# First and last K block loaded in halves, unread TensorE products, and softmax denominators moved ahead, in a cached attention decode kernel

## The chip, the cores and the metric

The kernel runs on one core of one Trainium2 chip. The metric is device microseconds of one launch, as the median of several runs. Beside the runs there is one profiled execution, from which all rows below come; times in it are counted from the first instruction, and the span reaches to the last one.

## The reference

Two tokens (B = 2, one step each, D = 512) pass through attention with a cached K and V of 8192 positions, 32 heads of 128, and the result is gated by a small MLP:

```python
xn = layernorm(x)
q = (xn @ wq)                       # 2 x 32 heads x 128
scores = q . k_cache * Dh**-0.5     # 2 x 32 x 8192
p = softmax(scores)
o = p . v_cache
s = o.reshape(2, 1, 4096) @ wo
g = silu(gelu(layernorm(xn) @ w1 + b1) @ w2 + b2)
return x + s * g
```

Everything is float32. K and V are 268 MB each, wo and wq 8.4 MB each: every byte is used once.

## The kernel before, in words

The 64 (token, head) pairs are taken two at a time, in N = 32 rounds. In a round, partitions 0 to 63 hold one head's 8192 positions (128 each) and partitions 64 to 127 the other's; a round's K, and its V, is one block of 128 partitions x 128 positions x 128 numbers, 8.4 MB. There are three such buffers, `big[0..2]`: two for K (`KBUF`), one for V (`VB`). The setup uses `big[2]` for the MLP weights and `big[1]` for wq; in the end the last V (number 31) goes into `KBUF[0]`, and wo into `VB`.

The order on each engine is written out by hand. Semaphores carry the dependences: `op` issues one instruction with its waits, `take` waits on a semaphore and counts it down. The code of almost every instruction is in the helper `op` (L51 in the rows), so rows are told apart by tiles.

- SP issues all large transfers into one queue: the MLP weights, wq, K 0, K 1 (after the product with wq, L265), V 0 (L288), and then in round n the block K n+2, which waits until VectorE is through with K n (`k_done`, L297), and V n+1, which waits until TensorE is through with V n (`p_v`, L298). In round 30 come the two halves of V 31, each with its own semaphore (L301), and in L302 to L305, after the product with V 30, wo in seven pieces (`WO_CUTS`).
- VectorE in round n: K times the query in place (L276), the sum over the 128 numbers of each position (L277), the maximum of each partition `MX` (L279), and, from TensorE's transpose of `MX`, the negated maximum of each head `nm` (L280). It does the next K only after `nm`.
- TensorE in round n (`softmax`, `weighted`): the transpose of `MX`, the product that spreads `nm` over the partitions (`pn`), then 32 products of the exponentials `PZ` with V (two records each in the trace, on four groups of 32 output rows), and four products that bring the result O into columns (`pt`). Its 31 rounds after the first are a loop on the engine (L412); the last V is done by `weighted(KBUF[0], last=True)`, which waits for each half of V 31 before the products that read it.
- ScalarE copies `pn` to `bias`, makes the exponentials with their sums (`RS`), and copies O out of PSUM (`o4`, `OT`).

After the last round VectorE makes `Z` (O spread for the gathering product, L310) and `ZL` (the sums `RS` spread likewise, L313); TensorE makes from them the unnormalised rows and the denominators in `OA` (L417 to L421); VectorE takes the reciprocal of the denominators `rl` (L315) and normalises (`on`, L316). Then TensorE runs 128 products with wo (256 records, L422), waiting for each piece of wo where it is first read, and VectorE gates the sum, adds x (`res`, L318) and the result is stored.

Of the kernel before, what the change touches and what calls it, by code (L numbers as in the profile page):

```python
# [4 lines left out]
AF = mybir.ActivationFunctionType  # L5
ALU = mybir.AluOpType
AX = mybir.AxisListType
# [6 lines left out]
class Program:  # L14
# [24 lines left out]
    def wait(self, eng, *tokens):  # L39
        for name, v in self.need(eng, tokens):  # L40
            self.engines[eng].wait_ge(self.sem(name), v)

    def take(self, eng, name, v=1):

        self.engines[eng].wait_ge(self.sem(name), v).then_inc(self.sem(name), -v)  # L45

    def op(self, eng, method, *args, waits=(), sig=None, quiet=False, **kwargs):
        need = self.need(eng, waits)
        for name, v in need[:-1]:
            self.engines[eng].wait_ge(self.sem(name), v)  # L50
        ins = getattr(self.engines[eng], method)(*args, **kwargs)  # L51
        for name, v in need[-1:]:
            ins._wait_ge(self.sem(name), v)
        if quiet:
            return None
        name = sig or "own_" + eng
        by = 16 if method == "dma_start" else 1
        ins.then_inc(self.sem(name), by)
        self.counts[name] += by
        return name, self.counts[name]  # L60


def decode_kernel(nc, x, kc, vc, wq, wo, w1, b1, w2, b2, out):
    P = 128
    B, H, S, DH = kc.shape
# [17 lines left out]
    PH = P // H  # L83
    OC = DH // PH
    BH = B * H
    NPB = 512 // DH
    WO_CUTS = (0, 10, 18, 24, 28, 30, 31, 32)
    V_CUTS = (0, KP // 2, KP)

    pr = Program(nc)  # L90
    op, wait, take = pr.op, pr.wait, pr.take
# [7 lines left out]
    kf = kc.rearrange("b h s d -> (b h s d)").rearrange("(n p j d) -> n p j d", p=P, j=KP, d=DH)  # L99
# [4 lines left out]
    KBUF, VB = rows[:2], rows[2]  # L104
# [32 lines left out]
    z = sb([P, P], "z")  # L137
# [6 lines left out]
    SC = [sb([P, KP], f"sc{i}") for i in range(2)]  # L144
# [42 lines left out]
    op("SP", "dma_start", b1_sb[:, NF:], b1[F - P:, None], sig="d_b")  # L187
    t["b"] = op("SP", "dma_start", b2_sb, b2[None, :], sig="d_b")
    op("SP", "dma_start", wq_sb, wq.rearrange("(p c) n -> p c n", p=P), sig="d_wq")
    k_land = {0: op("SP", "dma_start", KBUF[0], kf[0], sig="d_k0")}  # L190
    t["x4m"] = op("DVE", "memset", x4, 0.0)
    for b in range(B):
        t["x4"] = op("ACT", "dma_start", x4[b::R, :], x[b, 0].rearrange("(j n) -> j n", n=P), sig="d_x4",
# [68 lines left out]
    t["th"] = op("ACT", "activation", th, z, AF.Tanh, scale=0.5, waits=[t["z"]])  # L262


    op_k1 = op("SP", "dma_start", KBUF[1], kf[1], sig="d_k1", waits=[pe("pq"), ("d_wq", 16)])  # L265
    k_land[1] = op_k1

    pending = {}
    for n in range(N):
        k = KBUF[n % U]  # L270
        if n:

            op("ACT", "copy", o4, po, sig="s_o4", waits=[pe_n("p_v", n - 1)])
            t["OT"] = op("ACT", "copy", OT[:, U * (n - 1):U * n], pt[:, :U], waits=[pe_n("p_t", n - 1)])
        qb = Q[:, n, :].unsqueeze(1).to_broadcast([P, KP, DH])
        a = op("DVE", "tensor_tensor", out=k, in0=k, in1=qb, op=ALU.mult, waits=[k_land[n], Qt[n]])  # L276
        a = op("DVE", "tensor_reduce", out=SC[n % 2], in_=k, axis=AX.X, op=ALU.add, waits=[a], sig="v_k")  # L277
        k_done = a
        op("DVE", "tensor_reduce", out=MX, in_=SC[n % 2], axis=AX.X, op=ALU.max, waits=[a], sig="v_mx")  # L279
        op("DVE", "tensor_reduce", out=nm, in_=pm[:1, :P].rearrange("o (s r) -> o s r", s=U), axis=AX.X,  # L280
           op=ALU.max, negate=True, waits=[pe_n("p_m", n)], sig="v_nm")
        if n == 0:
            a = op("DVE", "scalar_tensor_tensor", gate, th, 1.0, z, op0=ALU.add, op1=ALU.mult,
                   waits=[t["th"], t["pool"]])
            t["gate"] = a

            wait("SP", t["sel"], t["qnat"], pe("pgate"))
            op("SP", "dma_start", VB, vf[0], sig="d_v")  # L288
        a = op("ACT", "copy", bias, pn[:, :1], waits=[pe_n("p_n", n)])
        sc = SC[n % 2].rearrange("p (t j) -> p t j", j=JW)  # L290
        for s in range(U):
            r = slice(HP * s, HP * (s + 1))
            op("ACT", "activation", PZ[r, :, s, :], sc[r], AF.Exp, bias=bias[r], scale=SCALE,
               accum_out=RS[r, n:n + 1], waits=[a, t["pool"]], sig="s_pz")
        m = n + 2
        if m < N:
            k_land[m] = op("SP", "dma_start", KBUF[m % U], kf[m], sig=f"d_k{m % U}", waits=[k_done])  # L297
            op("SP", "dma_start", VB, vf[m - 1], sig="d_v", waits=[pe_n("p_v", m - 2)])  # L298
        elif m == N:
            for i, (c0, c1) in enumerate(zip(V_CUTS, V_CUTS[1:])):  # L300
                op("SP", "dma_start", KBUF[m % U][:, c0:c1], vf[N - 1][:, c0:c1], sig=f"d_v31{i}", waits=[k_done])  # L301
            wait("SP", pe_n("p_v", N - 2))  # L302
            wo_v = wo.rearrange("(p c) n -> p c n", p=P)
            for i, (c0, c1) in enumerate(zip(WO_CUTS, WO_CUTS[1:])):
                op("SP", "dma_start", wo_sb[:, c0:c1], wo_v[:, c0:c1], sig=f"d_wo{i}")  # L305
    op("ACT", "copy", o4, po, sig="s_o4", waits=[pe_n("p_v", N - 1)])
    t["OT"] = op("ACT", "copy", OT[:, U * (N - 1):], pt[:, :U], waits=[pe_n("p_t", N - 1)])

    shape = [P, BH, PH]
    op("DVE", "tensor_tensor", out=Z, in0=blk.unsqueeze(1).to_broadcast(shape),  # L310
       in1=OT.unsqueeze(2).to_broadcast(shape), op=ALU.mult, waits=[t["OT"], t["blk"]])
    shape = [P, N, U * PH]
    t["Z"] = op("DVE", "tensor_tensor", out=ZL, in0=half.unsqueeze(1).to_broadcast(shape),  # L313
                in1=RS.unsqueeze(2).to_broadcast(shape), op=ALU.mult, waits=[t["half"]])
    a = op("DVE", "reciprocal", rl, OA[:, :, OC], waits=[pe_n("p_oa", 0)])  # L315
    t["on"] = op("DVE", "tensor_tensor", out=on, in0=OA[:, :, :OC], in1=rl.unsqueeze(2).to_broadcast([P, B, OC]),  # L316
                 op=ALU.mult, waits=[a])
# [11 lines left out]
    def mm(dst, w, v, start=True, stop=True, sig=None, waits=(), skip=False):  # L329
        kw = {"skip_group_check": True} if skip else {}  # L330
        if sig in PE_EVENTS:
            done.append(sig)
            sig = "pe_setup"
        return op("PE", "matmul", dst, w, v, start=start, stop=stop, waits=waits, sig=sig, quiet=sig is None, **kw)
# [49 lines left out]
           waits=[t["b"]], sig="pgate" if j == QT - 1 else None)  # L384
    assert done == PE_EVENTS, done

    def softmax():
        take("PE", "v_mx")
        op("PE", "transpose", pm[:1, :P], MX, ident, sig="p_m")
        take("PE", "v_nm")  # L390
        for s in range(U):
            mm(pn[HP * s:HP * (s + 1), :1], srow, nm[:, s:s + 1], sig="p_n" if s == U - 1 else None)

    def weighted(v, last=False):
        take("PE", "s_pz", U)
        if not last:
            take("PE", "d_v", 16)
        for i in range(NT):
            if last and i * JW in V_CUTS:
                nc.tensor.wait_ge(pr.sem(f"d_v31{V_CUTS.index(i * JW)}"), 16)  # L400
            j = i % QT
            mm(po[R * j:R * j + U * JW, :], PZ[:, i].rearrange("p s j -> p (s j)"),
               v[:, i * JW:(i + 1) * JW, :].rearrange("p j d -> p (j d)"), start=i < QT, stop=i + QT >= NT,
               sig="p_v" if i == NT - 1 else None)
        take("PE", "s_o4")
        for i in range(JW):
            mm(pt[:, :U], o4[:, i * DH:(i + 1) * DH], mod[:, i:U * JW:JW], start=i == 0, stop=i == JW - 1,
               sig="p_t" if i == JW - 1 else None)

    wait("PE", t["mem"], t["pool"], t["mod"])  # L410
    softmax()
    with nc.tensor.Fori(0, N - 1):  # L412
        weighted(VB)
        softmax()
    weighted(KBUF[0], last=True)

    for b in range(B):  # L417
        h = slice(b * H, (b + 1) * H)
        mm(OA[:, b, :OC], Z[:, h].rearrange("p h r -> p (h r)"), mod, waits=[t["Z"]])
        m = slice(b * HH, (b + 1) * HH)  # L420
        mm(OA[:, b, OC:], ZL[:, m].rearrange("p n r -> p (n r)"), ones[:, :1], sig="p_oa" if b == B - 1 else None)  # L421
# [32 lines left out]
```

## Time and profile before

| | us |
|---|---|
| median of 3 runs (lowest, highest) | 1304.08 (1302.92, 1304.64) |
| profiled execution, its own time | 1304.39 |
| its span | 1303.1 |
| VectorE busy | 1129.3 (87%) |
| TensorE busy | 404.0 (31%) |
| ScalarE busy | 70.5 (5%) |
| bytes moved, mean rate over the span | 559.5 MB, 429 GB/s |

The profile is one page of sums and a trace that can be asked for a stretch of time. A row of the timeline has the start, the duration, the engine, the line, the operation with its tiles and shapes, and in brackets how long the engine had been idle before it and what ended that. "PEld" is TensorE's weight load, "SPq" the issue of a transfer. The mean TensorE clock granted in the span was 0.633 of the full one. Of a transfer the trace has the time from its issue to its landing.

### The profile page before, as it was taken

Reading aid. Unit: us, or ns where it says so; the run is one execution under the profiler, and the core shown is the slowest. Engines: PE = TensorE matmul, PEld = TensorE weight load, DVE = VectorE, ACT = ScalarE, POOL = GpSimd, SP = SyncE. Lnnn points to the kernel's source line nnn. Section 1 sums busy time; section 2 is a strip of 40 time slices with the busy share of each in tenths; the row PEclk is TensorE's granted clock in tenths of the full one; section 3 lists DMA queues with packets and bytes.
Section 4 is the critical chain, followed back from the end, with each engine's and each line's share of the span. In section 5 each row is a group of like instructions: output and inputs, shape, how many; then the busy total and the mean of one; then the engine's idle time right before and its main releaser. Section 6 shows DMA issues by size and latency. Waiting matters only on the chain. (4 is left out here: it accounts for less than half of the span.)

```text
span 1303.1 us, 7007 instructions
## 1 busy us (share of the span) xinstructions
PE 404.0 (31%) x3128; PEld 147.0 (11%) x3128; DVE 1129.3 (87%) x166; ACT 70.5 (5%) x244; POOL 1.1 (0%) x8
## 2 busy tenths in 40 slices
PE   6602333212333311333321233221233331133337
PEld 6300010000001000100000010000011000001103
DVE  2299999998889988888988888988888998888891
ACT  1200000000000000000000000000000000000000
POOL 0000000000000000000000000000000000000000
PEclk9956666556666656666656666655666655666667
DMA  9999999999999999999999999999999999999997
GB/s 401 444 424 437 429 437 431 433 433 435 433 431 437 433 437 433 435 433 437 428 439 429 439 429 435 433 431 437 431 439 431 437 431 439 429 439 429 439 420 311
DMA packets 11280, 559.51 MB, mean 429 GB/s; under 512 B 1523, under 2 KB 1539, under 8 KB 2054
## 3 DMA queue, kind: packets, MB, share of 16 engines
q1 hardware_dynamic: 11242, 559.36, 99.4%
q8 instruction: 6, 0.10, 0.0%
q14 instruction: 4, 0.03, 0.0%
q10 hardware_dynamic: 28, 0.01, 0.0%
HBM read 559.37 MB, written 0.00 MB: 429 GB/s over the span
## 5 line engine op out<-in xcount | busy, mean ns | idle before, releaser
L51 DVE TENSOR_TENSOR big<-big,Q 128x16384 f32<-128x16384 f32 x32 | 551.1, 17222 | 102.1 <-DMA big<-in_A_k_cache_dram 77.1
L51 DVE TENSOR_REDUCE sc<-big 128x128 f32<-128x16384 f32 x32 | 551.0, 17220 | 1.1
L51 PE MATMUL bank<-big,PZ 128*8 128x512 f32 x2048 | 293.0, 736 | 618.3 <-PEq L45 618.3
L51 PEld LDWEIGHTS bank<-big,PZ 128*8 128x8 f32 x2048 | 60.7, 103 | 823.7 <-issue 823.7
L51 PE MATMUL bank<-ident,MX 128*1 128x128 f32 x32 | 11.9, 371 | 217.8 <-PEq L45 217.8
L51 ACT COPY o<-bank 128x512 f32<-128x512 f32 x32 | 18.7, 585 | 874.0 <-PE bank L51 874.0
L51 PE MATMUL bank<-mod,o 128*128 128x2 f32 x256 | 32.8, 250 | 25.6 <-PEq L45 25.6
L51 PEld LDWEIGHTS bank<-mod,o 128*128 128x128 f32 x256 | 31.0, 191 | 54.4 <-issue 54.4
L51 PEld LDWEIGHTS bank<-ident,MX 128*1 128x1 f32 x32 | 2.5, 79 | 219.8 <-issue 219.8
L51 ACT ACTIVATE PZ<-sc,bias 64x128 f32<-64x128 f32 x64 | 25.5, 399 | 1.9
L51 DVE TENSOR_REDUCE nm<-bank 1x2 f32<-1x128 f32 x32 | 8.9, 278 | 17.8 <-PE bank L51 17.8
L51 PE MATMUL bank<-yT,big 128*128 128x2 f32 x88 | 19.9, 364 | 0.8 <-DMA big<-in_B_w_dram 0.8
L51 PEld LDWEIGHTS bank<-yT,big 128*128 128x128 f32 x88 | 19.9, 321 | 0.9 <-DMA big<-in_B_w_dram 0.9
L51 DVE TENSOR_TENSOR gh<-bank,b_sb 128x22 f32<-128x22 f32 x1 | 0.2, 182 | 21.6 <-PE bank L51 21.6
L51 ACT COPY bias<-bank 128x1 f32<-128x1 f32 x32 | 5.1, 159 | 250.9 <-PE bank L51 250.9
L51 PE MATMUL bank<-nm,srow 1*64 1x1 f32 x128 | 12.0, 243 | 14.8 <-PEq L45 14.8
L51 PEld LDWEIGHTS bank<-nm,srow 1*64 1x64 f32 x128 | 10.2, 200 | 24.1 <-issue 24.1
L51 DVE TENSOR_TENSOR Z<-blk,OT 128x256 f32<-128x256 f32 x1 | 0.4, 424 | 13.9 <-ACT OT L51 13.9
L51 PE MATMUL bank<-big,xnT 128*2 128x512 f32 x64 | 9.7, 773 | 7.3 <-DMA big<-in_A_wq_dram 7.3
L51 ACT ACTIVATION_READ_ACCUMULATOR PZ<-sc,bias 64x1 f32 x64 | 11.8, 185 | 0.0
L51 DVE TENSOR_REDUCE MX<-sc 128x1 f32<-128x128 f32 x32 | 9.2, 286 | 1.1
L51 PE MATMUL bank<-big,on 128*2 128x128 f32 x256 | 9.2, 317 | 0.6 <-DVE on L51 0.6
(65 smaller groups left out, 65.7 us busy)
## 6 DMA issues: line engine op xcount, KB each, us to landing
big<-in_A_v_cache_dram SPq DMA_DIRECT2D x2, 4096.0 KB, 37.9
big<-in_B_w_dram SPq DMA_DIRECT2D x1, 2752.0 KB, 9.4
big<-in_B_w_dram SPq DMA_DIRECT2D x1, 2560.0 KB, 14.8
big<-in_A_wo_dram SPq DMA_DIRECT2D x1, 2560.0 KB, 16.6
big<-in_A_wo_dram SPq DMA_DIRECT2D x1, 2048.0 KB, 21.1
big<-in_A_wo_dram SPq DMA_DIRECT2D x1, 1536.0 KB, 24.3
big<-in_A_wo_dram SPq DMA_DIRECT2D x1, 1024.0 KB, 25.9
big<-in_A_k_cache_dram SPq DMA_DIRECT2D x32, 42.9
```

The source lines that it names most:

```text
L51: ins = getattr(self.engines[eng], method)(*args, **kwargs)
```

## The change

There are three parts.

1. K 0 and K 31 are loaded by two transfers each, of half the positions, with a semaphore for each half (`load_k`, `K_CUTS`); VectorE multiplies and sums each half by itself. The other K blocks stay whole. V 31 was in halves before.
2. `unread(4, 2)` and the like issue TensorE products of the identity with 512, 256 or 128 columns of the queries `Q` into bank 6, which nobody reads. They stand in every round before the transpose of `MX` (twice 512 columns) and before the `nm` product (128 columns), and in the end before the last exponentials, between the halves of V 31, before the O transposes, before the `OA` products and before the wo products. The first one also waits until the gate has been copied out of bank 6.
3. `ZL`, the two products that make the denominators, and their reciprocal are put ahead: VectorE makes `ZL` after the last `nm`, as soon as the last exponentials are done, TensorE makes the denominators right after the last V products (`p_den`), and the reciprocal follows. `Z`, the two row products and the normalisation stay where they were.

```diff
-    V_CUTS = (0, KP // 2, KP)
+    HALVES = (0, KP // 2, KP)
+    WHOLE = (0, KP)
+    K_CUTS = {0: HALVES, N - 1: HALVES}
...
+    def load_k(n, *waits):
+        cuts = K_CUTS.get(n, WHOLE)
+        k_land[n] = [op("SP", "dma_start", KBUF[n % U][:, a:b], kf[n][:, a:b], sig=f"d_k{n % U}{i}", waits=waits)
+                     for i, (a, b) in enumerate(zip(cuts, cuts[1:]))]
...
-        a = op("DVE", "tensor_tensor", out=k, in0=k, in1=qb, op=ALU.mult, waits=[k_land[n], Qt[n]])
-        a = op("DVE", "tensor_reduce", out=SC[n % 2], in_=k, axis=AX.X, op=ALU.add, waits=[a], sig="v_k")
+        cuts = K_CUTS.get(n, WHOLE)
+        for i, (c0, c1) in enumerate(zip(cuts, cuts[1:])):
+            qb = Q[:, n, :].unsqueeze(1).to_broadcast([P, c1 - c0, DH])
+            a = op("DVE", "tensor_tensor", out=k[:, c0:c1], in0=k[:, c0:c1], in1=qb, op=ALU.mult,
+                   waits=[k_land[n][i], Qt[n]])
+            a = op("DVE", "tensor_reduce", out=SC[n % 2][:, c0:c1], in_=k[:, c0:c1], axis=AX.X, op=ALU.add,
+                   waits=[a], sig="v_k")
...
+    t["ZL"] = op("DVE", "tensor_tensor", out=ZL, in0=half.unsqueeze(1).to_broadcast(shape),
+                 in1=RS.unsqueeze(2).to_broadcast(shape), op=ALU.mult, waits=[t["pz"], t["half"]])
+    t["rl"] = op("DVE", "reciprocal", rl, OA[:, :, OC], waits=[pe_n("p_den", 0)])
     op("ACT", "copy", o4, po, sig="s_o4", waits=[pe_n("p_v", N - 1)])
...
-    t["Z"] = op("DVE", "tensor_tensor", out=ZL, in0=half.unsqueeze(1).to_broadcast(shape),
-                in1=RS.unsqueeze(2).to_broadcast(shape), op=ALU.mult, waits=[t["half"]])
-    a = op("DVE", "reciprocal", rl, OA[:, :, OC], waits=[pe_n("p_oa", 0)])
+    t["Z"] = op("DVE", "tensor_tensor", out=Z, in0=blk.unsqueeze(1).to_broadcast(shape),
+                in1=OT.unsqueeze(2).to_broadcast(shape), op=ALU.mult, waits=[t["OT"], t["blk"]])
...
+    def unread(*heads):
+
+        for n in heads:
+            mm(bank[6][:, :n * DH], ident, Q[:, :n, :].rearrange("p n d -> p (n d)"), waits=[t["z"], t["Q0"]])
+
     def softmax():
+        unread(4, 4)
         take("PE", "v_mx")
         op("PE", "transpose", pm[:1, :P], MX, ident, sig="p_m")
+        unread(1)
         take("PE", "v_nm")
...
-        take("PE", "s_pz", U)
+        if last:
+            unread(4, 2)
+            wait("PE", t["pz"])
+        else:
+            take("PE", "s_pz", U)
...
+            if last and i * JW == HALVES[1]:
+                unread(2)
...
+        if last:
+            for b in range(B):
+                m = slice(b * HH, (b + 1) * HH)
+                mm(OA[:, b, OC:], ZL[:, m].rearrange("p n r -> p (n r)"), ones[:, :1], waits=[t["ZL"]],
+                   sig="p_den" if b == B - 1 else None)
+            unread(1)
         take("PE", "s_o4")
...
     weighted(KBUF[0], last=True)
+    unread(2)
...
+    unread(1)
     for i, (c0, c1) in enumerate(zip(WO_CUTS, WO_CUTS[1:])):
```

More of the change, by code (lines that the diff above doesn't have):

```diff
@@ L189, in decode_kernel @@
     op("SP", "dma_start", wq_sb, wq.rearrange("(p c) n -> p c n", p=P), sig="d_wq")
-    k_land = {0: op("SP", "dma_start", KBUF[0], kf[0], sig="d_k0")}
+    def load_k(n, *waits):
+        cuts = K_CUTS.get(n, WHOLE)
+        k_land[n] = [op("SP", "dma_start", KBUF[n % U][:, a:b], kf[n][:, a:b], sig=f"d_k{n % U}{i}", waits=waits)
+                     for i, (a, b) in enumerate(zip(cuts, cuts[1:]))]
+    k_land = {}
+    load_k(0)
     t["x4m"] = op("DVE", "memset", x4, 0.0)
@@ L262, in decode_kernel @@
     t["th"] = op("ACT", "activation", th, z, AF.Tanh, scale=0.5, waits=[t["z"]])
-    op_k1 = op("SP", "dma_start", KBUF[1], kf[1], sig="d_k1", waits=[pe("pq"), ("d_wq", 16)])
-    k_land[1] = op_k1
+    load_k(1, pe("pq"), ("d_wq", 16))
     pending = {}
@@ L274, in decode_kernel @@
             t["OT"] = op("ACT", "copy", OT[:, U * (n - 1):U * n], pt[:, :U], waits=[pe_n("p_t", n - 1)])
-        qb = Q[:, n, :].unsqueeze(1).to_broadcast([P, KP, DH])
-        a = op("DVE", "tensor_tensor", out=k, in0=k, in1=qb, op=ALU.mult, waits=[k_land[n], Qt[n]])
-        a = op("DVE", "tensor_reduce", out=SC[n % 2], in_=k, axis=AX.X, op=ALU.add, waits=[a], sig="v_k")
+        cuts = K_CUTS.get(n, WHOLE)
[5 more added lines that the diff above has]
+                   waits=[a], sig="v_k")
         k_done = a
@@ L292, in decode_kernel @@
             r = slice(HP * s, HP * (s + 1))
-            op("ACT", "activation", PZ[r, :, s, :], sc[r], AF.Exp, bias=bias[r], scale=SCALE,
-               accum_out=RS[r, n:n + 1], waits=[a, t["pool"]], sig="s_pz")
+            t["pz"] = op("ACT", "activation", PZ[r, :, s, :], sc[r], AF.Exp, bias=bias[r], scale=SCALE,
+                         accum_out=RS[r, n:n + 1], waits=[a, t["pool"]], sig="s_pz" if n < N - 1 else None)
         m = n + 2
         if m < N:
-            k_land[m] = op("SP", "dma_start", KBUF[m % U], kf[m], sig=f"d_k{m % U}", waits=[k_done])
+            load_k(m, k_done)
             op("SP", "dma_start", VB, vf[m - 1], sig="d_v", waits=[pe_n("p_v", m - 2)])
         elif m == N:
-            for i, (c0, c1) in enumerate(zip(V_CUTS, V_CUTS[1:])):
+            for i, (c0, c1) in enumerate(zip(HALVES, HALVES[1:])):
                 op("SP", "dma_start", KBUF[m % U][:, c0:c1], vf[N - 1][:, c0:c1], sig=f"d_v31{i}", waits=[k_done])
@@ L305, in decode_kernel @@
                 op("SP", "dma_start", wo_sb[:, c0:c1], wo_v[:, c0:c1], sig=f"d_wo{i}")
+    shape = [P, N, U * PH]
+    t["ZL"] = op("DVE", "tensor_tensor", out=ZL, in0=half.unsqueeze(1).to_broadcast(shape),
+                 in1=RS.unsqueeze(2).to_broadcast(shape), op=ALU.mult, waits=[t["pz"], t["half"]])
+    t["rl"] = op("DVE", "reciprocal", rl, OA[:, :, OC], waits=[pe_n("p_den", 0)])
     op("ACT", "copy", o4, po, sig="s_o4", waits=[pe_n("p_v", N - 1)])
@@ L309, in decode_kernel @@
     shape = [P, BH, PH]
-    op("DVE", "tensor_tensor", out=Z, in0=blk.unsqueeze(1).to_broadcast(shape),
-       in1=OT.unsqueeze(2).to_broadcast(shape), op=ALU.mult, waits=[t["OT"], t["blk"]])
-    shape = [P, N, U * PH]
-    t["Z"] = op("DVE", "tensor_tensor", out=ZL, in0=half.unsqueeze(1).to_broadcast(shape),
-                in1=RS.unsqueeze(2).to_broadcast(shape), op=ALU.mult, waits=[t["half"]])
-    a = op("DVE", "reciprocal", rl, OA[:, :, OC], waits=[pe_n("p_oa", 0)])
+    t["Z"] = op("DVE", "tensor_tensor", out=Z, in0=blk.unsqueeze(1).to_broadcast(shape),
+                in1=OT.unsqueeze(2).to_broadcast(shape), op=ALU.mult, waits=[t["OT"], t["blk"]])
     t["on"] = op("DVE", "tensor_tensor", out=on, in0=OA[:, :, :OC], in1=rl.unsqueeze(2).to_broadcast([P, B, OC]),
-                 op=ALU.mult, waits=[a])
+                 op=ALU.mult, waits=[t["rl"], pe_n("p_oa", 0)])
     a = op("DVE", "scalar_tensor_tensor", res, acc, 0.5, gate, op0=ALU.mult, op1=ALU.mult,
@@ L398, in weighted @@
         for i in range(NT):
-            if last and i * JW in V_CUTS:
-                nc.tensor.wait_ge(pr.sem(f"d_v31{V_CUTS.index(i * JW)}"), 16)
+            if last and i * JW == HALVES[1]:
+                unread(2)
+            if last and i * JW in HALVES:
+                nc.tensor.wait_ge(pr.sem(f"d_v31{HALVES.index(i * JW)}"), 16)
             j = i % QT
@@ L408, in weighted @@
                sig="p_t" if i == JW - 1 else None)
-    wait("PE", t["mem"], t["pool"], t["mod"])
+    wait("PE", t["mem"], t["pool"], t["mod"], t["z"])
     softmax()
@@ L415, in decode_kernel @@
     weighted(KBUF[0], last=True)
+    unread(2)
     for b in range(B):
         h = slice(b * H, (b + 1) * H)
-        mm(OA[:, b, :OC], Z[:, h].rearrange("p h r -> p (h r)"), mod, waits=[t["Z"]])
-        m = slice(b * HH, (b + 1) * HH)
-        mm(OA[:, b, OC:], ZL[:, m].rearrange("p n r -> p (n r)"), ones[:, :1], sig="p_oa" if b == B - 1 else None)
+        mm(OA[:, b, :OC], Z[:, h].rearrange("p h r -> p (h r)"), mod, waits=[t["Z"]],
+           sig="p_oa" if b == B - 1 else None)
+    unread(1)
     for i, (c0, c1) in enumerate(zip(WO_CUTS, WO_CUTS[1:])):
```

## The prediction

> **What bounds the kernel now.** I read the page first, then the chain that ended last, then the timeline of the last 70 us with the landings of its transfers, and the TensorE clock microsecond by microsecond. All times are us from the start of the span.
>
> ```profile
> span 1303.1 us, 7007 instructions
> q1 hardware_dynamic: 11242, 559.36, 99.4%
> L51 DVE TENSOR_TENSOR big<-big,Q 128x16384 f32<-128x16384 f32 x32 | 551.1, 17222 | 102.1 <-DMA big<-in_A_k_cache_dram 77.1
> ```
>
> One queue carries 559.36 MB and fills 99.4% of the span of the 16 DMA engines. VectorE waits 77.1 us for K. So the body of the kernel is the transfer stream, and only what stands after the stream's last byte, or what makes the stream pause, can change the time.
>
> The end is different. The chain view, its last 16 us (start, duration, what):
>
> ```profile
> 1287.82 0.42 DVE Z L51
> 1288.25 0.35 DVE ZL L51
> ...
> 1288.64 1.88 PE bank L51 x8
> ...
> 1290.55 0.18 DVE rl L51
> ...
> 1290.75 0.24 DVE on L51
> ...
> 1291.12 9.27 PE bank L51 x256
> 1300.41 0.30 DVE res L51
> ```
>
> The last piece of TensorE is the product with wo: 256 records without a pause, up to 1300.4. The issue rows and the landings of the last two pieces of wo (us from issue to landing; the second landing row is the median of both):
>
> ```profile
> 1269.12 0.43 SPq L51 DMA_DIRECT2D big<-in_A_wo_dram  x1
> 1269.59 0.43 SPq L51 DMA_DIRECT2D big<-in_A_wo_dram  x1
> big<-in_A_wo_dram SPq DMA_DIRECT2D x1, 256.0 KB, 27.0
> big<-in_A_wo_dram SPq DMA_DIRECT2D x2, 256.0 KB, 27.2
> ```
>
> The sixth piece lands at 1269.12 + 27.0 = 1296.1; the median 27.2 makes the seventh 27.4, so it lands at 1297.0. TensorE is 3.4 us behind its data there: the end is not the stream but the chain before the wo products. That chain, from the timeline:
>
> ```profile
> 1199.55 17.23 DVE L51 TENSOR_TENSOR big<-big,Q 128x16384 f32<-128x16384 f32 x1 [3.06 <-DMA big<-in_A_k_cache_dram]
> ...
> 1234.91 0.28 DVE L51 TENSOR_REDUCE nm<-bank 1x2 f32<-1x128 f32 x1 [0.56 <-PE bank L51]
> 1238.27 17.23 DVE L51 TENSOR_TENSOR big<-big,Q 128x16384 f32<-128x16384 f32 x1 [3.09 <-DMA big<-in_A_k_cache_dram]
> 1267.30 1.02 PE L51 MATMUL bank<-mod,o 128*128 128x2 f32 x8 [0.80 <-PEq L45]
> 1272.79 0.29 DVE L51 TENSOR_REDUCE MX<-sc 128x1 f32<-128x128 f32 x1
> 1273.22 0.37 PE L51 MATMUL bank<-ident,MX 128*1 128x128 f32 x1 [4.90 <-PEq L45]
> 1275.81 9.96 PE L51 MATMUL bank<-big,PZ 128*8 128x512 f32 x64 [1.38 <-PEq L45]
> ```
>
> The last K lands at 1238.27 after VectorE has stood idle 3.09 us; its scores are complete at 1272.79; the last V product runs 1275.81 to 1285.77.
>
> **First K in halves: nothing.**
>
> ```profile
> 51.67 0.59 ACT L51 COPY Q<-bank 128x512 f32<-128x512 f32 x1 [1.19 <-PE bank L51]
> 56.77 17.22 DVE L51 TENSOR_TENSOR big<-big,Q 128x16384 f32<-128x16384 f32 x1 [24.93 <-ACT Q L51]
> 91.27 0.33 SPq L51 DMA_DIRECT2D big<-in_A_k_cache_dram  x1
> 95.78 9.47 PE L51 MATMUL bank<-big,PZ 128*8 128x512 f32 x64 [2.86 <-PEq L45]
> ```
>
> VectorE could start at 52.3, when the first queries are copied, instead of 56.77, so it is done with K 0 some 4.3 us earlier, and K 2 is issued near 87 instead of 91.27. But at 91.27 the transfer of V 0 still had 4.5 us to go (its product starts at 95.78), so the queue was not empty then either. The stream covers the whole gain. The extra issue costs SP 0.4 us while wq is still in flight.
>
> **Last K in halves: 2.7 us on the chain.** The halves of the last V show what a half does in this queue:
>
> ```profile
> 1228.43 0.33 SPq L51 DMA_DIRECT2D big<-in_A_v_cache_dram  x1
> big<-in_A_v_cache_dram SPq DMA_DIRECT2D x1, 29.2
> 1234.43 0.43 SPq L51 DMA_DIRECT2D big<-in_A_v_cache_dram  x1
> big<-in_A_v_cache_dram SPq DMA_DIRECT2D x1, 4096.0 KB, 33.3
> big<-in_A_v_cache_dram SPq DMA_DIRECT2D x1, 4096.0 KB, 42.6
> 1300.81 0.29 DVE L51 TENSOR_TENSOR res<-res,x 128x128 f32<-128x128 f32 x1
> ```
>
> V 30 lands at 1257.6, the second half of V 31 at 1234.43 + 42.6 = 1277.0, and the first half, issued 0.4 earlier, 9.7 us before it, at 1267.4. So the first half of K 31 will be there near 1238.2 - 9.7 = 1228.5, and VectorE starts when it is free, at 1234.91 + 0.28 = 1235.2: 3.05 us earlier. Four instructions stand for two: from 0.29 us for 128 elements and 17.23 for 16384 an instruction has a fixed part of 0.16, so two more cost 0.35 with their gaps. The maximum moves from 1272.79 to 1270.1. The split itself: V 31's two halves took 1277.0 - 1257.6 = 19.4 us, and K 30 and K 31 start 38.72 us apart, with two transfers in between (19.36 each), so a cut costs the stream 0 to 0.2 us; I take 0.1 in all.
>
> **Unread products.** No row shows a 128-wide weight with 512 columns. The nearest are the V products, four records side by side on 32 output rows each:
>
> ```profile
> 1276.62 0.17 PEld L51 LDWEIGHTS bank<-big,PZ 128*8 128x8 f32 x4 [0.69 <-issue]
> 1282.16 0.10 PEld L51 LDWEIGHTS bank<-big,PZ 128*8 128x8 f32 x4 [0.32 <-issue]
> 1195.80 0.37 PE L51 MATMUL bank<-ident,MX 128*1 128x128 f32 x1 [3.74 <-PEq L45]
> ```
>
> A set of four takes 0.17 + 0.69 = 0.86 us at the half clock and 0.42 at the full one, and each product has two records. If a full-width record lasts like a set, one product of 512 costs 0.85 (full) to 1.7 us (half); if it shared like a quarter, 0.2. The pair in softmax costs 1.7 to 3.4 us. In the loop TensorE sits 3.74 us idle before the transpose (rows like the third one), so even 3.4 us is covered, and what it overran would first eat the 3.09 us that VectorE waits for K. In the last round the maximum is due at 1270.4 and the O transposes end at 1268.3: 1.7 us fits, 3.4 delays the transpose by 1.2. The product of 128 columns (0.2 to 0.4) lies in the 0.46 us before the next row. The 4 and 2 heads before the last exponentials cost 1.3 to 2.6 in an idle time of 1.38. I take the full clock, because the product before it has just ended, and keep 2.4 us of delay for the bound.
>
> What they are to gain is the clock (columns: stretch, length, busy TensorE, weights, DVE, ACT, POOL, clock, DMA share, GB/s):
>
> ```profile
> 1271.00:1272.00 1.00, 0.00 (x0) 0.00 (x0) 1.00 (x1) 0.00 (x0) 0.00 (x0) 0.74 0.93 401
> 1281.00:1282.00 1.00, 1.00 (x12) 0.15 (x8) 0.00 (x0) 0.00 (x0) 0.00 (x0) 0.64 1.03 438
> 1288.00:1289.00 1.00, 0.36 (x2) 0.36 (x2) 0.58 (x2) 0.00 (x0) 0.00 (x0) 0.77 0.96 406
> 1295.00:1296.00 1.00, 1.00 (x36) 0.82 (x32) 0.00 (x0) 0.00 (x0) 0.00 (x0) 0.82 0.26 94
> 367.44 8.47 PE L51 MATMUL bank<-big,PZ 128*8 128x512 f32 x64 [22.01 <-PEq L45]
> ```
>
> It falls at 1271.5, rises at 1281.7, falls at 1288.5, rises at 1295.4: the V product ran 5.9 us at half clock, the wo product 4.2. At the full clock throughout, the V product would take 16 sets x 0.43 = 6.9 us instead of 9.96; in another round it took 8.47, by its luck with the clock. The four changes lie 10.2, 6.8 and 6.8 us apart, multiples of 3.41.
>
> The Trainium skill, "TensorE: Matmul & The Clock Gate" (Part 1), says that a free-running window of 3413 ns decides the clock, which rises after a busy window and falls after an idle one; the spacing above agrees. By that rule unread products keep the clock up only if nearly every window is filled, and the time of before itself floats from run to run by the window's phase while a kernel that ends with its transfers does not.
>
> **The end, added up.** Maximum 1270.1, V product from 1270.1 + 3.0 (as from 1272.79 to 1275.81) = 1273.1. First half at the full clock 3.4: 1276.5; the second half waits for its V until 1277.0 and ends at 1280.5. The two denominators' products (4 of the 8 records that took 1.88: 0.94) go before the O transposes, 0.3 more than the copy of O hides, with 0.2 of unread: O transposed at 1282.8 (before: 1.8 us after the V product, now 2.3). Then Z 0.42, with copies and gaps 1283.4; two products of 0.47 each: 1284.4; the normalisation 0.24: wo begins near 1284.9 instead of 1291.12. ZL (0.35), the reciprocal (0.18 and a gap) and two products are off the chain: 1.5 us less, 0.5 more. With every bound against it (2.4 us of delay, the first half at half clock, 3.4) it begins near 1289.
>
> At 1284.9 wo has landed only in part. Its 256 records, 27 ns each at the full clock (four abreast, 128 columns), need 6.8 us, so TensorE now waits for each piece and the end is the last landing: 1297.0, plus 0.1 for the cut, plus 8 records: 0.5 (full clock) to 0.85 (half): 1297.7. From there to the end of the span it was 1303.1 - 1300.4 = 2.7: **span 1300.4**, 2.7 less. The profiled execution took 1304.39, 1.29 over its span: 1301.7. It lies 0.3 above the median 1304.08 of the runs shown, so against that: **1301.4**, -0.2%.
>
> **Rivals.** 0.2% (2.6 us) is about what a measurement of this kernel can tell from no change, so the line is 1301.5.
> - The stream bounds the end, 1300.6 to 1302.4 by its own scatter: 0.73, of which three fifths lie under the line.
> - TensorE still ends last (clock not held, unread products in the way): wo begins at 1289, runs up to 6.3 us at the half clock and ends near 1299: span 1301.8, 1302.8 against the median. The change would then not do what it says about the clock, and most of the gain would stay, since the K halves alone give 2.7: 0.13.
> - The stream closes a pause somewhere at the start because K 2 is issued earlier: up to 0.7 less, 1300.7. Against it: the queue was never empty. 0.08.
> - Slower: the softmax pair holds the transpose, the transpose holds VectorE's next K, and each round loses. It needs the pair to exceed 3.74 + 3.09 = 6.8 us, four times the full-clock price; at 7 us it costs 0.2 x 31 = 6 us less the gain: 1308. The rows of 0.86 us for a set speak against it: 0.04.
> - Each cut of a transfer costs the stream 2 us: 1305.4. V 31 in two halves at 19.4 us speaks against it: 0.02. The Trainium skill, "DMA: Bandwidth & Descriptors" (Anatomy of one DMA), has a fixed 2.0 us per transfer; in a queue that stays filled this trace shows no such step.
>
> So faster 0.73 x 0.6 + 0.08 = 0.52; same 0.29 + 0.13 + 0.02 = 0.44; slower 0.04. Range 1300.4 to 1303.3: from the short stream to the case where TensorE ends last.
>
> **What would show it.** VectorE's last K starting near 1235 without a wait for DMA; the V product in two runs with a pause up to 1277; TensorE waiting for DMA inside the wo products; reciprocal and ZL before 1281. The forecast is wrong if the wo products still run without pauses to the end, if rounds take longer than 38.7 us, or if the last piece of wo lands more than 1 us from 1297.1.

## The result, and the profile after

The changed kernel takes 1301.08 us (median of 17 runs, 1300.7 to 1302.37) against 1303.61 for the kernel before (17 runs, 1301.66 to 1305.48): ratio 0.9982, 95% interval 0.9975 to 0.999. The forecast was 1301.4. The profiled execution took 1301.08, its span 1299.8. The gain is 2.5 us, and the runs of the changed kernel lie within 1.7 us of each other where those of before spread over 3.8.

The page of the changed kernel: the span, the row of the new products, and the chain that ended last by line.

```profile
span 1299.8 us, 7423 instructions
...
DMA big<-in_A_wo_dram 2%; PE bank L51 1%; SPq L51 0%; DVE res L51 0%; DVEq L50 0%
...
L51 PE MATMUL bank<-Q,ident 128*128 128x512 f32 (+2 forms) x204 | 80.3, 503 | 0.5 <-ACT z L51 0.5
```

The end of its chain view (start, duration, what):

```profile
1269.96 26.63 DMA big<-in_A_wo_dram
...
1296.63 0.45 PE bank L51 x8
...
1297.10 0.30 DVE res L51
```

Before, the chain ended with 9.27 us of wo products that ran without a pause. Now it ends with the last transfer: the seventh piece of wo is issued near 1269.96 and lands at 1296.6, eight records follow it, and the rest is as before. TensorE has become a follower of the stream. The timeline of the end, TensorE and VectorE (start, duration, engine, line, operation, and in brackets the idle time before and what ended it):

```profile
1234.40 8.67 DVE L51 TENSOR_TENSOR big<-big,Q 128x8192 f32<-128x8192 f32 x1
...
1268.56 1.96 PE L51 MATMUL bank<-Q,ident 128*128 128x512 f32 x4
...
1269.14 0.29 DVE L51 TENSOR_REDUCE MX<-sc 128x1 f32<-128x128 f32 x1
...
1270.36 0.27 PE L51 MATMUL bank<-ident,MX 128*1 128x128 f32 x1
...
1272.85 3.62 PE L51 MATMUL bank<-big,PZ 128*8 128x512 f32 x32
...
1277.03 3.62 PE L51 MATMUL bank<-big,PZ 128*8 128x512 f32 x32
...
1284.22 2.37 PE L51 MATMUL bank<-big,on 128*2 128x128 f32 x80
...
1287.51 1.92 PE L51 MATMUL bank<-big,on 128*2 128x128 f32 x61 [0.92 <-DMA big<-in_A_wo_dram]
...
1291.64 1.49 PE L51 MATMUL bank<-big,on 128*2 128x128 f32 x48 [1.19 <-DMA big<-in_A_wo_dram]
...
1294.17 1.06 PE L51 MATMUL bank<-big,on 128*2 128x128 f32 x32 [1.03 <-DMA big<-in_A_wo_dram]
1295.39 1.01 PE L51 MATMUL bank<-big,on 128*2 128x128 f32 x24 [0.17 <-DMA big<-in_A_wo_dram]
...
1296.63 0.40 PE L51 MATMUL bank<-big,on 128*2 128x128 f32 x8 [0.23 <-DMA big<-in_A_wo_dram]
```

VectorE starts the last K straight after `nm`, without the 3.09 us of waiting; the maximum comes at 1269.14 instead of 1272.79; the last V product is two runs of 3.62 us instead of one of 9.96, with an unread product between them (the second half of V 31 had landed near 1276.5, when the first run ended); and the wo products wait for at least five of their seven pieces. The clock (the eighth column) is at its full value in every microsecond from 1263 to 1300, also while TensorE waits; two of these rows:

```profile
1273.00:1274.00 1.00, 1.00 (x12) 0.22 (x8) 0.07 (x1) 0.00 (x0) 0.00 (x0) 1.00 0.66 283
...
1290.00:1291.00 1.00, 0.39 (x3) 0.09 (x2) 0.00 (x0) 0.00 (x0) 0.00 (x0) 1.00 1.01 422
```

### The profile page after: what moved, and what is told of

Its sections match the earlier page's. It is cut to its first block, busy times and chain, and to the rows that moved or that the text cites. A ratio compares the mean times of both kernels' runs of the same rounds, so it can differ in the third digit from the quotient of the medians.

```text
span 1299.8 us, 7423 instructions
## 1 busy us (share of the span) xinstructions
PE 468.5 (36%) x3332; PEld 173.5 (13%) x3332; DVE 1129.8 (87%) x170; ACT 70.5 (5%) x244; POOL 1.1 (0%) x8
## 5 line engine op out<-in xcount | busy, mean ns | idle before, releaser
L51 DVE TENSOR_TENSOR big<-big,Q 128x16384 f32<-128x16384 f32 (+1 forms) x34 | 551.4, 16217 | 100.3 <-DMA big<-in_A_k_cache_dram 81.1
L51 DVE TENSOR_REDUCE sc<-big 128x128 f32<-128x16384 f32 (+1 forms) x34 | 551.3, 16216 | 1.2
L51 PE MATMUL bank<-Q,ident 128*128 128x512 f32 (+2 forms) x204 | 80.3, 503 | 0.5 <-ACT z L51 0.5
L51 PE MATMUL bank<-ident,MX 128*1 128x128 f32 x32 | 9.1, 285 | 124.8 <-PEq L45 124.8
L51 PEld LDWEIGHTS bank<-Q,ident 128*128 128x128 f32 x204 | 34.3, 196 | 17.8 <-issue 17.7
```

## The experiments

All variants are cut from the changed kernel. Every median is of 11 runs. Within one table block the kernels ran on the same chip beside the same runs of the kernel before.

| kernel | median (lowest, highest), us | to before (95%) |
|---|---|---|
| last K in halves alone | 1302.23 (1301.48, 1302.95) | 0.9987 (0.9978, 0.9996) |
| unread products alone | 1304.22 (1301.59, 1305.24) | 1.0 (0.9991, 1.0009) |
| denominators ahead alone | 1302.55 (1301.04, 1304.26) | 0.9994 (0.9985, 1.0003) |
| first K in halves alone | 1302.58 (1300.89, 1303.80) | 0.999 (0.9981, 0.9999) |
| before, 33 runs | 1303.93 (1301.61, 1305.48) | |
| | | |
| changed kernel again | 1301.19 (1300.73, 1301.44) | 0.9986 (0.9977, 0.9995) |
| changed, no unread products | 1301.61 (1300.82, 1302.09) | 0.9986 (0.9977, 0.9995) |
| changed, last K whole | 1301.82 (1300.65, 1302.65) | 0.9988 (0.9979, 0.9997) |
| changed, first K whole | 1302.26 (1301.23, 1303.34) | 0.9998 (0.9989, 1.0007) |
| before, 33 runs | 1303.09 (1301.59, 1305.02) | |
| | | |
| changed, first K landed in halves, summed whole | 1301.68 (1301.01, 1302.76) | 0.9985 (0.9976, 0.9994) |
| changed, 4 products more before wo | 1301.14 (1300.36, 1301.59) | 0.9982 (0.9973, 0.9991) |
| changed, 12 products more before wo | 1305.78 (1304.80, 1307.91) | 1.0017 (1.0008, 1.0026) |
| changed, 12 products in each loop round | 1305.25 (1303.92, 1305.79) | 1.0009 (1.0, 1.0018) |
| before, 33 runs | 1303.56 (1302.07, 1304.95) | |

The ratio is not the quotient of the two medians: it differs from it by up to 0.0005, which is 0.6 us. Each interval is about 1.2 us to either side. So what a part is worth is known to about a microsecond, and the traces have to say the rest. The changed kernel itself did not run in the third block; the run with four more products, whose end proves to be the same, stands for it there.

The theory to be tested (S): the end is the last landing of wo plus 3.2 us, and a part is worth something only until TensorE's chain is under that. The rival (A): the parts are separate savings that add up to 2.5 us.

### The last K in halves, alone

```diff
-    K_CUTS = {0: HALVES, N - 1: HALVES}
+    K_CUTS = {N - 1: HALVES}
...
     def unread(*heads):
-        for n in heads:
+        for n in ():
```

and the denominators put back to where they were before.

> Only the last K in halves; no unread products, denominators late, first K whole. Theory S (the end is the landing of the last piece of wo plus 3.2 us, and each part only has to bring TensorE's chain under that): the last K starts at about 1235 without a wait for DMA, the maximum comes 2.7 us earlier than in before (about 1270), the last V product still runs at mixed clock (about 9.5 us), wo products begin near 1288 and end near 1297.5; time 1.5 to 2.3 us under before, about as good as the whole change. Rival A (the three parts add up to the 2.5 us): the half costs 0.35 in two more instructions and the V product waits for its own second half, so it is worth 1 us or less.

Timeline of this kernel:

```profile
1236.56 8.67 DVE L51 TENSOR_TENSOR big<-big,Q 128x8192 f32<-128x8192 f32 x1
...
1274.03 8.53 PE L51 MATMUL bank<-big,PZ 128*8 128x512 f32 x64 [1.29 <-ACT PZ L51]
...
1287.10 5.78 PE L51 MATMUL bank<-big,on 128*2 128x128 f32 x144 [0.61 <-DVE on L51]
...
1298.28 0.40 PE L51 MATMUL bank<-big,on 128*2 128x128 f32 x8 [0.23 <-DMA big<-in_A_wo_dram]
```

As S has it: no wait for the last K, wo products from 1287.1, and the end set by the last landing, just before 1298.28. This execution's stream was late by 1.65 us against the changed kernel's (1296.63). Its median gain is 1.7 us, inside what S expected; what is missing to 2.5 is the late stream, taken up below.

### The unread products, alone

```diff
-    K_CUTS = {0: HALVES, N - 1: HALVES}
+    K_CUTS = {}
```

and the denominators put back.

> Only the unread products; K blocks whole, denominators late. Theory S: the V product of the last round starts near 1275.8 as before, runs at the full clock in about 7 us with a small pause, the rest of the chain is shorter by the clock too, wo products begin near 1288 at the full clock and wait for the last pieces; time 2 to 2.5 us under before, as the whole change. Rival A: about 1 us under before. Rival L (unread products hold up the loop): rounds longer than 38.7 us, time over before.

Timeline, and one row of the clock:

```profile
1268.36 1.96 PE L51 MATMUL bank<-Q,ident 128*128 128x512 f32 x4
...
1272.58 0.37 PE L51 MATMUL bank<-ident,MX 128*1 128x128 f32 x1 [2.26 <-PEq L45]
...
1273.73 2.92 PE L51 MATMUL bank<-Q,ident 128*128 128x512 f32 x4
...
1276.58 4.93 PE L51 MATMUL bank<-big,PZ 128*8 128x512 f32 x32
...
1290.23 5.40 PE L51 MATMUL bank<-big,on 128*2 128x128 f32 x141
```

```profile
1272.00:1273.00 1.00, 0.42 (x3) 0.45 (x3) 0.41 (x3) 0.00 (x0) 0.00 (x0) 0.73 0.69 295
```

S missed: no gain at all. The pair lasts 1.96 us, then TensorE is idle for 2.26 until the maximum of the whole last K comes, and in that hole the clock falls (0.73 in this microsecond, 0.50 in the next). So the four and two heads behind it run at half clock (the row of the first four takes 2.92 us instead of the 1.55 of the changed kernel) and put the V product off; it still has its first half at mixed clock (4.93 instead of 3.62). In the changed kernel the halves bring the maximum 3 us earlier, the pair fills the whole gap, and the clock holds. In the two profiles without the halves, this one and the one with the last K whole below, the products did not hold it.

### The denominators ahead, alone

```diff
-    K_CUTS = {0: HALVES, N - 1: HALVES}
+    K_CUTS = {}
...
     def unread(*heads):
-        for n in heads:
+        for n in ():
```

> Only the denominators ahead. Theory S: the chain before the wo products is 1.0 to 1.5 us shorter, clock as in before, so wo products run on to the end without waiting for DMA to any extent; time 0.7 to 1.5 us under before, hard to tell from no change. Rival A: 0.5 to 1 us as well; this run alone does not tell the two apart, their sum with the others does (S: the single gains add up to 4 us or more; A: to 2.5).

```profile
1275.59 9.33 PE L51 MATMUL bank<-big,PZ 128*8 128x512 f32 x64 [1.29 <-ACT PZ L51]
...
1288.93 9.56 PE L51 MATMUL bank<-big,on 128*2 128x128 f32 x256 [0.41 <-DVE on L51]
```

From the end of the V product (1284.92) to wo it takes 4.0 us here, 5.35 before: 1.3 us less, where 1.0 was worked out, and wo then runs without a pause to the end. The median is 1.4 us under before, the ratio says 0.8, and its interval includes 1.

### The first K in halves, alone

```diff
-    K_CUTS = {0: HALVES, N - 1: HALVES}
+    K_CUTS = {0: HALVES}
...
     def unread(*heads):
-        for n in heads:
+        for n in ():
```

and the denominators put back.

> Only the first K in halves. Theory S: VectorE starts 4.5 us earlier (near 52), K 2 is issued near 87, and the landing of the last piece of wo does not move by more than its own scatter (1 us); time as before within 0.6 us. Rival F (the earlier start closes a pause in the stream): the last piece of wo lands 0.5 us or more earlier, time 0.5 to 0.7 us under before.

```profile
1290.38 9.22 PE L51 MATMUL bank<-big,on 128*2 128x128 f32 x256 [0.61 <-DVE on L51]
```

The median is 1.35 us under before, outside S's 0.6 and in F's direction, with an interval that ends just under 1. TensorE's chain still ends last here (the wo products run without a pause), so the gain comes through it: the last maximum is taken at 1272.12 instead of 1272.79. The spread is wide (2.9 us), as it is in before.

### Each part taken out: unread products

```diff
     def unread(*heads):
-        for n in heads:
+        for n in ():
```

> The changed kernel without its unread products. Theory S (the end is the last landing of wo plus 3.2 us; a part is worth something only until TensorE's chain is under the stream): the last V product starts near 1273 and takes 8.5 to 10 us at mixed clock, wo products begin near 1286, wait for the last pieces of wo, and the time is that of the changed kernel within 0.4 us. Rival U (the products carry a part of the gain): wo products run on without waiting for DMA, time 0.7 us or more over the changed kernel.

```profile
1272.17 8.98 PE L51 MATMUL bank<-big,PZ 128*8 128x512 f32 x64 [1.29 <-ACT PZ L51]
...
1284.73 2.37 PE L51 MATMUL bank<-big,on 128*2 128x128 f32 x80 [0.41 <-DVE on L51]
...
1296.83 0.40 PE L51 MATMUL bank<-big,on 128*2 128x128 f32 x8 [0.23 <-DMA big<-in_A_wo_dram]
```

The V product starts 0.7 us earlier than in the changed kernel (no products ahead of the transpose and of the exponentials) and takes 8.98 instead of 7.8 with its pause; wo starts 0.5 us later and the end is again the last landing. The median is 0.42 us over the changed kernel, where S allowed 0.4 and U asked for 0.7: nearly nothing, and too little to be told from none.

### The last K whole

```diff
-    K_CUTS = {0: HALVES, N - 1: HALVES}
+    K_CUTS = {0: HALVES}
```

> The changed kernel with the last K whole. Theory G (unread products hold the clock only where the gap they fill is about as short as they are; with the last K whole 2 us stay empty before the last transpose): the clock is at half when the last V product starts, the 4 and 2 heads before it run at half clock and put it off by about 1 us (start near 1276.5), so the products cost there what they give later; wo products start at 1288.5 to 1289.5, time 0.5 to 1.5 us over the changed kernel and more scattered. Rival S-only (the products hold the clock in any gap): V product in two runs of 3.6 us, wo products near 1286 with waits for DMA, time that of the changed kernel.

```profile
1272.60 0.27 PE L51 MATMUL bank<-ident,MX 128*1 128x128 f32 x1 [2.87 <-PEq L45]
...
1275.43 4.91 PE L51 MATMUL bank<-big,PZ 128*8 128x512 f32 x32
...
1288.09 5.76 PE L51 MATMUL bank<-big,on 128*2 128x128 f32 x141
```

G's reading with smaller numbers: TensorE is idle for 2.87 us before the last transpose, the clock falls again before the last V product (0.83 of full between 1274 and 1275, 0.50 in the next three microseconds), wo starts at 1288.1, soon at half clock, and its products end at 1297.8; 0.6 us over the changed kernel, with a spread of 2.0 us against 0.7.

So the parts do not seem to add up: alone they gain 1.7, 0, 1.4 and 1.35 by the medians, together 2.5 and not 4.4, and taking out the unread products or the halves of the last K costs only 0.4 and 0.6. By the ratios the parts sum to 3.8 us, and the four intervals of 1.2 us together reach down to the gain of the whole, so the sum alone does not refute A. What does is the delay of four products below, which costs nothing.

### The first K whole

```diff
-    K_CUTS = {0: HALVES, N - 1: HALVES}
+    K_CUTS = {N - 1: HALVES}
```

> The changed kernel with the first K whole. Theory S: the stream never ran empty, so nothing is lost: time that of the changed kernel within 0.4 us, last landing of wo within 1 us of its 1296.6. Rival F (the earlier K 2 spares the stream small pauses in the first rounds; the first K alone in halves was 1.3 us under before): 0.7 to 1.3 us over the changed kernel, with longer rounds among the first ten.

```profile
1296.79 0.40 PE L51 MATMUL bank<-big,on 128*2 128x128 f32 x8 [0.23 <-DMA big<-in_A_wo_dram]
```

1.07 us over the changed kernel: F. Of the 1.90 us that the changed kernel gains in this block, 0.83 are left by the medians and 0.3 by the ratio. The profiled execution was one of the fastest of this kernel (1301.23), so its last landing is only 0.16 us late, and the row does not show the loss. This was the part I had at nothing, and it is the one whose loss costs most. Next comes the cause.

### The first K landed in halves, but summed whole

```diff
-        cuts = K_CUTS.get(n, WHOLE)
+        cuts = K_CUTS.get(n, WHOLE) if n else WHOLE
         for i, (c0, c1) in enumerate(zip(cuts, cuts[1:])):
...
-                   waits=[k_land[n][i], Qt[n]])
+                   waits=(k_land[n] if n == 0 else [k_land[n][i]]) + [Qt[n]])
```

> The changed kernel, its first K still in two transfers, but multiplied and summed whole after both have landed, so that VectorE starts near 56.5 and K 2 is issued near 91.3 as in before. Theory L (the first K in halves is worth 1 us because K 2 is issued 9 us, not 4.4 us, before V 0 ends, so that no DMA engine runs out of work and starts K 2 with slow packets): time 0.5 to 1.2 us over the changed kernel, as with the first K whole (1302.3), and packets of well over 2.6 us near 93. Rival P (the smaller transfers themselves make it): time that of the changed kernel, 1301.2 within 0.4, and no slow packets there.

Issue of K 2 and the first two V products, of this kernel:

```profile
91.36 0.33 SPq L51 DMA_DIRECT2D big<-in_A_k_cache_dram  x1
...
95.66 9.61 PE L51 MATMUL bank<-big,PZ 128*8 128x512 f32 x64 [2.65 <-PEq L45]
...
135.03 5.27 PE L51 MATMUL bank<-big,PZ 128*8 128x512 f32 x32 [6.27 <-PEq L45]
```

and of the changed kernel:

```profile
86.05 0.33 SPq L51 DMA_DIRECT2D big<-in_A_k_cache_dram  x1
...
95.66 8.49 PE L51 MATMUL bank<-big,PZ 128*8 128x512 f32 x64 [7.96 <-PEq L45]
...
134.36 6.17 PE L51 MATMUL bank<-big,PZ 128*8 128x512 f32 x32 [10.92 <-PEq L45]
```

With K 2 issued at 91.36 the first round takes 39.37 us, with 86.05 it takes 38.70. The packet records of the traces, those of 64 KB that start between 84 and 100 us, say more (the usual duration is 2.42 us):

```
                            packets   over 2.7 us   longest, us
K 2 issued near 91 us:
  before                        105        4          3.86
  last K in halves alone        104       18          3.87
  unread products alone         105        6          4.01
  denominators ahead alone      104        1          2.74
  changed, first K whole        107        4          3.53
  changed, summed whole         105        4          4.11
K 2 issued at 86.0 to 87.5 us:
  the eight other traces    100-111        0          2.43
```

All eight traces with the early issue have none of these slow packets, all six with the late one have some (one of them a single one, just over 2.7), and they start at 93 to 98 us, when K 2's first packets do. No load of instructions falls between 84 and 100 us in any trace.

What it costs the stream can be added up. From the start of the product with V 0 to that with V 30 lie 30 rounds, 1161.0 us at 38.70 each. These two rows are the last in the two kernels above:

```profile
1257.50 8.96 PE L51 MATMUL bank<-big,PZ 128*8 128x512 f32 x64 [22.09 <-PEq L45]
...
1257.18 9.69 PE L51 MATMUL bank<-big,PZ 128*8 128x512 f32 x64 [22.29 <-PEq L45]
```

Here the rounds take 0.84 us more than 1161.0, in the changed kernel 0.52. Over all traces it is 0.4 to 2.5 us with the late issue (1.2 on average) and 0.2 to 0.5 with the early one (0.3): a difference of 0.8 us, about what the medians say. The time of this kernel, 1301.68, is 0.54 us over the run with four more products in its block; that is at the lower end of what theory L asked for (0.5 to 1.2) and little more than P allowed (0.4), so it is the packets and not the time that speak for L.

So the place is shown: the slow packets come where K 2 is issued only 4.2 to 4.5 us before the transfer ahead of it ends, and not where it is issued 8.7 us ahead or more; with the late issue they come whether K 0 was loaded in one transfer or, as here, in two. That it is the issue itself is argued: VectorE's product with K 1 and the first exponentials move with it by 5 us, and no run moved one without the other. How a few slow packets make up 0.8 us is argued too. In two profiles (this one and the last K in halves alone) the first round itself is longer by 0.7. Every other round of the 14 traces that is longer by more than 0.2 us, 1.5 at the most, holds a load of 8 or 16 KB of instructions on another queue, beside which a packet of 64 KB takes 2.7 to 3.1 us. In before the second round takes 39.43, with this load at 150.65:

```profile
q14 instruction: 1, 0.01, 4.8%
```

With the late issue such a load lengthens its round by up to 1.5 us, with the early one by 0.4 at the most. This fits engines that the slow packets have left behind, but these records do not say which engine moved a packet.

### Four and twelve products more before wo

```diff
-    unread(1)
+    unread(1, *[4] * 4)
     for i, (c0, c1) in enumerate(zip(WO_CUTS, WO_CUTS[1:])):
```

> The changed kernel with four more unread products of 512 columns (3.4 us at the full clock) right before the wo products. Theory S (the end is the last landing of wo): wo products begin near 1287.7 instead of 1284.2, their waits for DMA shrink, the end does not move: 1301.2 within 0.4. Rival (TensorE's chain still bounds the end): 3 us or more slower.

```profile
1288.53 5.42 PE L51 MATMUL bank<-big,on 128*2 128x128 f32 x192
...
1296.83 0.40 PE L51 MATMUL bank<-big,on 128*2 128x128 f32 x8 [0.23 <-DMA big<-in_A_wo_dram]
```

With twelve (`unread(1, *[4] * 12)`):

> The same with twelve (10.3 us). Theory S: TensorE has about 6 us to spare before the wo products (they need 6.8 us and may end at 1297), so 10.3 cost about 4.3 us: 1305.5, no waits for DMA left among the wo products. Rival: 10.3 us slower.

```profile
1294.57 7.17 PE L51 MATMUL bank<-big,on 128*2 128x128 f32 x256
```

4.3 us of delay cost nothing (1301.14 here, 1301.08 and 1301.19 for the changed kernel in the other sets); 10.3 us cost 4.6. TensorE has about 6 us to spare at the full clock, and the end is the stream's. S holds for the changed kernel, and A falls.

### Twelve products in each round of the loop

```diff
-    with nc.tensor.Fori(0, N - 1):
+    with nc.tensor.Fori(0, N - 2):
         weighted(VB)
-        softmax()
+        softmax(12)
+    weighted(VB)
+    softmax()
```

where the argument is the number of products of 512 columns before the transpose.

> The changed kernel with twelve unread products of 512 columns (10.3 us) instead of two before the transpose in all rounds but the first and the last. They overrun the 3.7 us of idle time by 6.6 us and so hold nm and VectorE's next K. Rival of the prediction (each round loses what exceeds 6.8 us): 3.5 us in some 28 rounds, about 98 us slower. Theory V (TensorE's place in a round is set by the landing of V, not by VectorE, so VectorE falls behind once, by 3 to 4 us, and no transfer is issued too late): rounds stay at 38.70 us, the time grows by 0 to 1.5 us.

```profile
1152.39 10.55 PE L51 MATMUL bank<-Q,ident 128*128 128x512 f32 x24
...
1162.78 0.27 PE L51 MATMUL bank<-ident,MX 128*1 128x128 f32 x1
...
1163.29 17.20 DVE L51 TENSOR_TENSOR big<-big,Q 128x16384 f32<-128x16384 f32 x1
...
1180.41 8.42 PE L51 MATMUL bank<-big,PZ 128*8 128x512 f32 x64 [16.62 <-PEq L45]
...
1219.11 9.54 PE L51 MATMUL bank<-big,PZ 128*8 128x512 f32 x64 [17.20 <-PEq L45]
...
1241.24 8.67 DVE L51 TENSOR_TENSOR big<-big,Q 128x8192 f32<-128x8192 f32 x1
...
1292.65 8.71 PE L51 MATMUL bank<-big,on 128*2 128x128 f32 x256
```

The 10.55 us hold the transpose and VectorE's next K, and yet a round is 38.70 us (1180.41 to 1219.11). V's landing sets when TensorE starts a round, so VectorE falls behind once and does not lose more; the transfers are issued far enough ahead. Only the last K pays: it starts at 1241.24 instead of 1234.40. The wo products begin at 1292.65 instead of 1284.22. About 6 of these 8.4 us are the ones that TensorE has to spare; the rest stays, and wo runs for its first 3.2 us at half clock (8.71 us instead of the 7.17 above). The time is 4.1 us over that of the run with four more products. Theory V holds for the rounds; it missed the time, with 0 to 1.5 us, since it had the lag at 3 to 4 us, and the last K starts 6.8 us late.

## Why the prediction was right, and where it was not

- **What bounds before and after.** Right: the chain before the wo products, then the last landing. The two runs with added products show the slack.
- **The last K.** Forecast: start 1235.2, maximum 1270.1. Measured: 1234.40 and 1269.14, in a stream that ran 0.6 us earlier (K 30 starts at 1198.94, before 1199.55). The start is right to 0.2 us and the maximum to 0.4.
- **Unread products, their size.** Right: a full-width record lasts like a set of four (0.43 us: 24 records in 10.55; the pair 1.96 with its tail). They do put off the last transpose, by 0.8 us, which I had at nothing at the full clock: the maximum came at 1269.14 where I had 1270.1, and the O transposes ended at 1268.7, not 1268.3. The slack hides it.
- **Unread products, their worth.** The text did not say that they depend on the halves; I had the clock held "because the product before it has just ended". With a hole of 2.26 us left it is not held. And in the changed kernel they are worth about 0.4 us, too little to be told from none, since the halves and the denominators bring the chain under the stream alone.
- **Denominators.** 1.5 less and 0.5 more; measured alone 1.3 us shorter. In the changed kernel wo began at 1284.22, forecast 1284.9. The reciprocal ran at 1281.22, 0.2 us after the 1281 that was named as its sign.
- **The end.** Forecast: last landing 1297.1 with the cut, 0.5 to 0.85 for eight records, 2.7 to the end. Measured: 1296.6, 0.47 and 2.7: span 1299.8 instead of 1300.4. The cut of the last K, taken at 0.1, costs 0.07: its round, from the product with V 29 to that with V 30, takes 38.78 us in the changed kernel (1218.40 to 1257.18) and 38.72 in before, and so in the other traces, 38.77 to 38.79 with the cut and 38.70 to 38.72 without.
- **The step that failed: "First K in halves: nothing."** "The queue was not empty" was true and not enough. The rival that an earlier K 2 closes a pause had the right trigger and a chance of 0.08; taking that part out costs 1.07 us, doing it with a late K 2 0.5. As far as one profile of each kernel goes, the missing term can be seen in the sum: the product with V 30 starts at 1257.74 in before, from which the sum takes the stream, and at 1257.18 in the changed kernel, and these 0.56 us are nearly all of the 0.6 by which the span came out too long. That the time came out only 0.3 too high is luck: the step from the profiled execution to the median took off another 0.3, and the profiled execution of the changed kernel is its median.
- **A bound that was added up wrongly.** The latest start of wo, given as 1289, is 1290.1 by its own terms (1270.1 + 2.4 of delay + 3.0 + 6.8 + 3.4 + 4.4), which would put the rival that TensorE still ends last, and with it the upper end of the range, about 1 us later. No run of the changed kernel came near it.
- **The slower rival.** Its mechanism was wrong, not only its chance: a round does not lose what the products overrun.

The Trainium skill, "TensorE: Matmul & The Clock Gate" (Part 1), on which the prediction leaned for the clock: that before floats with the phase of the window while a kernel that ends with its transfers does not agrees with the runs, 3.8 us of spread against 1.7 (0.7 in the second set). But not all of before's spread is the clock's: the changed kernel with the first K whole also ends with its transfers, and it spreads over 2.1 us. That the clock falls after an idle window is too narrow for the run with the unread products alone: there TensorE was busy until 1270.3 and idle for 2.26 us only, and the clock fell between 1272 and 1273. "DMA: Bandwidth & Descriptors" (Anatomy of one DMA): the fixed 2.0 us per transfer, which the section gives for transfers issued from GpSimd, does not show for these, issued from SP; the changed kernel has two transfers more, the cut of the last K costs 0.07 us, and the last landing is earlier.

## What to carry to other kernels

Find out first which of two late things ends last and by how much: here the chain was 3.4 us behind the last landing, and parts that save some 4 us one by one save 2.5 together. Filling TensorE's gaps kept its clock here only where the filling was about as long as the gap; in both runs that left two to three microseconds open it was lost. And a transfer queue that never runs empty can still lose time where a transfer is issued only a few microseconds before the one ahead of it ends, so an early step that "the stream covers" has to be looked at in the packets.

## What was not expected of the hardware

Among the first 64 KB packets of K 2 some took 2.7 to 4.1 us instead of 2.42 in all six traces in which it was issued near 91 us, and none over 2.43 in the eight with the issue at 86.0 to 87.5. The 16 engines' landings of one V block lie 1.5 to 3.5 us apart. This spread stays nearly the same from block to block; where a round is longer, by 0.2 to 1.5 us, it takes a new value and about keeps it, as it would if an engine that falls behind stayed behind. All but two of these rounds hold a load of 8 or 16 KB of instructions. What makes the first packets of K 2 slow stays open.
